# One decode step of attention beside a gated MLP: keys loaded three tiles ahead of values, and the stages spread over more iterations

## The chip, the cores and the metric

The kernel runs on one core of one Trainium2 chip. The core has a matrix engine (PE, whose weight loads the profile lists apart as PEld), a vector engine (DVE), a scalar engine (ACT), a general engine (POOL, hardly used here) and SP, the queue that issues the transfers. Sixteen DMA engines move data between the chip's memory (HBM) and the core's own memory (SBUF). PE writes its results to a second memory, PSUM.

The metric is the device time of one execution in microseconds. The kernel before has a median of 708.93 us over three runs (703.95 to 710.58).

## What is computed

```
x  = A_x                       # 4 batches, 1 token, D = 640
xn = layernorm(x)
q  = xn @ wq                   # 32 heads of 128 numbers
s  = q . k_cache * 128**-0.5   # for each batch and head: 4096 keys
p  = softmax(s)
o  = p . v_cache               # for each batch and head: 4096 values
A  = o @ wo
z  = gelu(xn @ w_in)           # 1728 columns, two halves of 864
z2 = layernorm(second half of z)
g  = w_sp * z2 + b_sp          # the sequence has length 1, so w_sp is one number
B  = (first half of z * g) @ w_out
out = x + A + B
```

All inputs are bf16. The two caches are 4 x 32 x 4096 x 128 numbers each, 268.4 MB together, and each number is used once. The weights are small beside them: wq and wo 5.2 MB each, w_in 2.2 MB, w_out 1.1 MB.

## The kernel before

**Tiles.** The work on the caches is cut into `NT` = 64 tiles. Tile i is one batch `b = i % 4` and one pair of heads `hp = i // 4`. Its keys lie in SBUF as 128 partitions x `NC` = 64 positions x 128 numbers (2 MB): the lower 64 partitions hold the first head, the upper 64 the second. Its values lie the same way. Key tiles, value tiles and, at the start, the three parts of wq all take their place from one pool of `KV_SLOTS` = 7 slots (line 16).

**One tile goes through these stages.**

- `stage_q` (L362): two matmuls spread the two rows of q over the partitions, and ACT copies the result (`qbc`).
- `products` (L380), twice, for a half of 32 positions each: DVE multiplies keys by q (L385). In the second half alone (`FOLDED`, L54) DVE then adds the upper 64 of the 128 products to the lower 64 (L394, "folding").
- `sums` (L398), twice: PE adds up groups of `RW` = 16 products by matmuls with an identity matrix, 512 columns each (L404): eight of them for the first half, four for the folded one. `row_sums` (L413), twice: DVE reduces the remaining 16 to one score (L414).
- The chain for the maximum: `lane_max` (DVE), `turn_max` (PE transposes), `head_max` (DVE, one maximum for each head), `spread_max` (L442; two matmuls, one for each head, with the constant `halves`, spread the two maxima over the partitions).
- `exps` (L454): ACT copies the maximum, and computes the exponentials of both heads and their sums.
- `weighted` (L470): 64 matmuls with the values as weights and the exponentials as the moving operand, "p.v" in what follows.

After every fourth tile (all batches of a head pair) come `group_den` (L488), `group_norm` (L497) and `group_proj` (L504, four matmuls with wo into the output's sum, `out_ps`).

**The order.** For PE, DVE and ACT the order of the instructions is written out by hand, in the loop of lines 529 to 551. Iteration i holds the products and sums of tile i, the maximum and the exponentials of tile i-1, and p.v of tile i-2. Each engine works through its own list in order, and waits at an instruction until that instruction's inputs are there.

**The loads** are all issued by SP, in the order of the program. `load_to(2 * i + KV_AHEAD)` (L531, with `KV_AHEAD` = 6) issues key and value tiles in turn: k0, v0, k1, v1, and so on. At iteration i these are k(i+2), which takes the slot that p.v of tile i-2 leaves, and v(i+2), which takes the slot of k(i-1). `load_wo` (L130) loads 640 KB of wo, enough for two head pairs, into one of two buffers. It is issued at iterations 1, 9, 17 and so on (L532). From iteration 9 on, the buffer that it takes is in use until the projection at the end of the following iteration, and SP waits in between.

At the start SP issues x, the two single numbers w_sp and b_sp (L77, L79), wq in three parts (L85), k0, v0, k1, v1, w_in (L139), w_out (L140) and the first part of wo.

**The query** (L203 to L216): eight groups of five matmuls, each with the 4 columns of xn as weights and 512 columns of wq as the moving operand, and a copy by ACT for each group.

**The gated MLP** hangs on single iterations (L351 to L356): the product with w_in in six parts of 15 matmuls at iterations 5 to 10 (`gmlp_z`; each has 96 columns of w_in, nine numbers apart, as weights, L239), the gelu at 11, the layer norm and the gate at 12, the product with w_out at 13. The nine chunks are of `FHC` = 96 columns, and w_out lies in SBUF as 96 partitions x 9 rows, so that each partition's rows are contiguous in HBM.

Of the kernel before, what the change touches and what calls it, by code (L numbers as in the profile page):

```python
# [9 lines left out]
FP32 = mybir.dt.float32  # L10
# [6 lines left out]
KV_AHEAD = 6  # L17
# [3 lines left out]
def kernel(  # L21
# [31 lines left out]
    RW = 16  # L53
    FOLDED = (1,)  # L54
    FHC = 96
    NFC = Fh // FHC
# [19 lines left out]
    wsp_bf = const.tile([1, 1], BF16)  # L76
    nc.sync.dma_start(out=wsp_bf[:], in_=B_w_sp[0:1, 0:1])  # L77
    bsp_bf = const.tile([1, 1], BF16)
    nc.sync.dma_start(out=bsp_bf[:], in_=B_b_sp[0:1].rearrange("(a b) -> a b", a=1))  # L79
# [30 lines left out]


    loads = []
    for i in range(NT - 2):
        loads += [("k", i), ("v", i)]
    loads += [("k", NT - 2), ("k", NT - 1), ("v", NT - 2), ("v", NT - 1)]
    n_loaded = [0]

    def load_to(n):
        while n_loaded[0] < min(n, len(loads)):
            what, i = loads[n_loaded[0]]  # L120
            if what == "k":
                load_k(i)
            else:
                load_v(i, 4 if i == NT - 1 else 1)
            n_loaded[0] += 1
# [4 lines left out]
    def load_wo(j):  # L130
        if j < H // HQ:
            wo_tiles[j] = wop.tile([P, HQ, D], BF16, name="wo")
            nc.sync.dma_start(out=wo_tiles[j][:], in_=wo_v[j])
# [20 lines left out]

    halves = const.tile([1, 2, P], FP32)
    nc.vector.memset(halves[:], 0.0)
    for hh in range(2):
        nc.vector.memset(halves[:, hh, hh * HALF : (hh + 1) * HALF], scale_qk)
# [44 lines left out]
    q_rows = const.tile([Bsz, HD], BF16)  # L203
    N0 = 512
    for j in range(HD // N0):
        q_ps = ps_m.tile([Bsz, N0], FP32, tag="m")
        for c in range(DC):
            t, i = wq_parts[c]
            nc.tensor.matmul(  # L209
                out=q_ps[:],  # L210
                lhsT=xnT[:, c, :],
                rhs=t[:, i, j * N0 : (j + 1) * N0],
                start=(c == 0),
                stop=(c == DC - 1),
            )
        nc.scalar.copy(out=q_rows[:, j * N0 : (j + 1) * N0], in_=q_ps[:])  # L216

# [12 lines left out]
    gm = {}  # L230

    def gmlp_z(k0, k1):
        if "z" not in gm:
            gm["z"] = ps_pv.tile([FHC, NZC, Bsz], FP32, tag="pv", name="zT")
        zT = gm["z"]
        w = w_in_sb[:].rearrange("p c (t f k) -> p c t k f", t=2, k=NFC)
        for k in range(k0, k1):
            for c in range(DC):
                nc.tensor.matmul(  # L239
                    out=zT[:, k, :],  # L240
                    lhsT=w[:, c, k // NFC, k % NFC, :],
                    rhs=xnT[:, c, :],
                    start=(c == 0),
                    stop=(c == DC - 1),
                )

    def gmlp_gelu():
        zz = work.tile([FHC, NZC, Bsz], FP32, name="zz")
        nc.vector.tensor_copy(out=zz[:], in_=gm["z"][:])
        gw = work.tile([FHC, NZC, Bsz], FP32, name="gw")  # L250
# [101 lines left out]
    for i in range(6):  # L352
        gmlp[5 + i] = lambda k0=3 * i: gmlp_z(k0, k0 + 3)
# [233 lines left out]
```

## Time and profile before

| | |
|---|---|
| median of three runs | 708.93 us (703.95 to 710.58) |
| the profiled execution | 699.59 us |
| its span, first to last instruction | 697.8 us |
| mean granted PE clock | 0.687 |
| busy: PE, DVE, ACT | 514.5, 482.1, 94.0 us |
| read from HBM | 282.24 MB |

The profile shows one execution. Its span leaves out 1.8 us that lie around the first and the last instruction. The parts that are used below are the shares of busy time; the span in 40 slices (a digit is the busy share in tenths, 9 is 90% or more; GB/s is what the DMA engines moved); the chain of work that ended last; the groups of instructions (line, engine, operation, output <- inputs, shapes, count, then the busy time and the mean of one in ns, then the engine's idle time just ahead of them and what ended most of it); the windows, which give each engine's busy time in a stretch of the span; the waits of the SP queue; and the order of time (start, duration, engine, line, operation, and in square brackets the idle time before it and what ended that).

Busy matmuls overlap in the pipeline, so that their mean duration is longer than the distance from one to the next.

### The profile page before, as it was taken

To read this page: it belongs to the slowest core of one execution; us is meant where nothing else is said; L and a number is where in the kernel's file an instruction comes from. 1 tells how busy PE (TensorE), PEld (TensorE's weight loads), DVE (VectorE), ACT (ScalarE), POOL (GpSimd) and SP (SyncE) were. 2 spreads that over 40 slices of the span, in tenths; PEclk is the share of its full clock that TensorE was granted. 3 is DMA by queue.
4 is the path that set the end of the run, shared out by engine and by line. 5 is a ranking of instruction groups with operands and counts; after the bars stand their busy time and mean duration, and the time that the engine had idled before them with its cause. 6 is when DMAs were issued, how large, how long until landed. Compare 5 with 4: busy or idle time off the path is not lost.

```text
span 697.8 us, 12619 instructions
## 1 busy us (share of the span) xinstructions
PE 514.5 (74%) x5601; PEld 291.5 (42%) x5601; DVE 482.1 (69%) x516; ACT 94.0 (13%) x400; POOL 1.4 (0%) x12
## 2 busy tenths in 40 slices
PE   3737689897697677686767858677676858778786
PEld 0213356564354344342444434344343424444354
DVE  1437667575779668676676857776697776769683
ACT  1210101012111101110110111011011101101111
POOL 0000000000000000000000000000000000000000
PEclk9965566665577758565586755767577665767656
DMA  8999999969999999999999999999999999999991
GB/s 351 431 368 423 427 425 428 425 265 425 427 428 425 399 429 426 427 426 401 429 427 425 397 424 428 426 427 390 428 428 425 429 385 429 425 429 426 425 420 47
DMA packets 23850, 283.06 MB, mean 406 GB/s; under 512 B 2316, under 2 KB 6420, under 8 KB 6932
## 3 DMA queue, kind: packets, MB, share of 16 engines
q1 hardware_dynamic: 23796, 282.26, 96.2%
q8 instruction: 44, 0.72, 0.4%
q14 instruction: 10, 0.08, 0.0%
HBM read 282.24 MB, written 0.01 MB: 404 GB/s over the span
## 4 chain that ended last, share of the span: by engine, by line
DMA 57%; PE 27%; DVE 14%; ACT 1%; issue 1%; SPq 1%; DVEq 0%
DMA k_nat<-in_A_k_cache_dram 55%; PE s_ps L404 15%; DVE prod L385 10%; PE pv L477 4%; PE zT L239 2%; DMA wq<-in_A_wq_dram 2%; PE nb_ps L445 2%; PE q_ps L209 1%; DVE prod L394 1%; PE out_ps L509 1%; DVE s_sb L414 1%; PE out_ps L343 1%; PE den L490 0%; ACT pm L461 0%; DVE nm L433 0%
## 5 line engine op out<-in xcount | busy, mean ns | idle before, releaser
L404 PE MATMUL s_ps<-prod,ident 128*128 128x512 bf16 x768 | 292.5, 542 | 112.7 <-DVE prod L385 112.6
L385 DVE TENSOR_TENSOR prod<-k_nat,qbc 128x4096 bf16<-128x4096 bf16 x128 | 291.5, 2278 | 107.4 <-DMA k_nat<-in_A_k_cache_dram 85.9
L404 PEld LDWEIGHTS <-ident 128*128 128x128 bf16 x768 | 90.7, 126 | 261.9 <-issue 240.8
L477 PEld LDWEIGHTS <-v_nat 128*128 128x128 bf16 x4096 | 116.8, 99 | 18.8 <-issue 12.8
L477 PE MATMUL pv<-pm,v_nat 128*128 128x2 bf16 x4096 | 114.2, 165 | 0.2 <-ACT pm L461 0.2
L414 DVE TENSOR_REDUCE s_sb<-s_ps 128x32 f32<-128x512 f32 x128 | 86.7, 677 | 3.9 <-PE s_ps L404 3.9
L445 PE MATMUL nb_ps<-nm,halves 1*128 1x1 f32 x256 | 47.5, 286 | 51.8 <-DVE nm L433 39.5
L378 ACT CAST qbc<-qbc_ps 128x128 bf16<-128x128 f32 x64 | 17.0, 266 | 477.8 <-PE qbc_ps L370 477.8
L394 DVE TENSOR_TENSOR prod<-prod 128x2048 bf16<-128x2048 bf16 x64 | 78.4, 1225 | 2.2
L445 PEld LDWEIGHTS nb_ps<-nm,halves 1*128 1x128 f32 x256 | 42.9, 235 | 60.7 <-issue 31.7
L461 ACT ACTIVATE pm<-s_sb,nb 64x64 bf16<-64x64 f32 x128 | 46.7, 365 | 2.9
L433 DVE TENSOR_REDUCE nm<-mT 1x2 f32<-1x128 f32 x64 | 17.6, 275 | 40.9 <-PE mT L428 40.7
L494 DVE RECIPROCAL rden<-den 128x8 f32<-128x8 f32 x16 | 3.3, 208 | 46.3 <-PE den L490 46.3
L461 ACT ACTIVATION_READ_ACCUMULATOR pm<-s_sb,nb 64x1 f32 x128 | 23.6, 185 | 0.0
L457 ACT COPY nb<-nb_ps 128x1 f32<-128x1 f32 x64 | 10.2, 159 | 95.3 <-PE nb_ps L445 95.3
L428 PE MATMUL mT<-ident_f,m 128*1 128x128 f32 x64 | 18.7, 292 | 0.0
L209 PE MATMUL q_ps<-wq,xnT 128*4 128x512 bf16 x40 | 13.5, 502 | 6.8 <-DMA wq<-in_A_wq_dram 6.6
L509 PE MATMUL out_ps<-wo,o_n 128*4 128x320 bf16 x64 | 17.4, 418 | 0.3 <-DVE o_n L499 0.3
L239 PEld LDWEIGHTS <-w_in_sb 128*96 128x96 bf16 x90 | 16.5, 268 | 2.5 <-issue 2.5
L370 PE MATMUL qbc_ps<-q_rows,ident 4*64 4x128 bf16 x128 | 16.3, 252 | 0.5 <-ACT q_rows L216 0.5
L239 PE MATMUL zT<-xnT,w_in_sb 128*96 128x4 bf16 x90 | 15.9, 307 | 0.0
L423 DVE TENSOR_REDUCE m<-s_sb 128x1 f32<-128x64 f32 x64 | 14.1, 220 | 2.2
(69 smaller groups left out, 69.8 us busy)
## 6 DMA issues: line engine op xcount, KB each, us to landing
k_nat<-in_A_k_cache_dram SPq DMA_DIRECT2D x64, 2048.0 KB, 21.5
v_nat<-in_A_v_cache_dram SPq DMA_DIRECT2D x63, 2048.0 KB, 17.9
wo<-in_A_wo_dram SPq DMA_DIRECT2D x8, 640.0 KB, 5.7
wq<-in_A_wq_dram SPq DMA_DIRECT2D x2, 2048.0 KB, 11.7
w_in_sb<-in_B_w_in_dram SPq DMA_DIRECT2D x1, 2160.0 KB
v_nat<-in_A_v_cache_dram SPq DMA_DIRECT2D x4, 512.0 KB, 13.0
w_out_sb<-in_B_w_out_dram SPq DMA_DIRECT2D x1, 1080.0 KB
wq<-in_A_wq_dram SPq DMA_DIRECT2D x1, 1024.0 KB, 13.7
```

What stands on the lines that cost most here:

```text
L209: nc.tensor.matmul(out=q_ps[:], lhsT=xnT[:, c, :], rhs=t[:, i, j * N0 : (j + 1) * N0], start=(c == 0), stop=(c == DC - 1),)
L239: nc.tensor.matmul(out=zT[:, k, :], lhsT=w[:, c, k // NFC, k % NFC, :], rhs=xnT[:, c, :], start=(c == 0), stop=(c == DC - 1),)
L385: nc.vector.tensor_tensor(out=t[:], in0=k_tiles[i][:, cs, :], in1=qbcs[i][:, None, :].to_broadcast([P, NH2, Dh]), op=ALU.mult,)
L394: nc.vector.tensor_tensor(out=t[:, :, 0:hd], in0=t[:, :, 0:hd], in1=t[:, :, hd:Dh], op=ALU.add)
L404: nc.tensor.matmul(out=s_ps[:], lhsT=ident[:], rhs=t[:, :, g * RW : (g + 1) * RW], start=(g == 0), stop=(g == n - 1),)
L414: nc.vector.tensor_reduce(out=scores[i][:, half * NH2 : (half + 1) * NH2], in_=sums_ps.pop((i, half))[:], axis=AX.X, op=ALU.add,)
L428: nc.tensor.transpose(out=mT[:], in_=maxes[i][:], identity=ident_f[:])
L433: nc.vector.tensor_reduce(out=nm[:], in_=maxes[i][:].rearrange("a (h p) -> a h p", h=2), axis=AX.X, op=ALU.max, negate=True,)
L445: nc.tensor.matmul(out=nb_ps[:], lhsT=halves[:, hh, :], rhs=maxes[i][:, hh : hh + 1], start=(hh == 0), stop=(hh == 1),)
L461: nc.scalar.activation(out=pm[ps, :, hh], in_=s_sb[ps, :], func=ACT.Exp, bias=nb[ps, :], scale=scale_qk, accum_out=a[ps, hh, b : b + 1],)
L477: nc.tensor.matmul(out=pvs[hp][:, :, b], lhsT=v_nat[:, c, :], rhs=pm[:, c, :], start=(c == 0), stop=(c == NC - 1),)
L509: nc.tensor.matmul(out=out_ps[:, oh, 0:NOH], lhsT=o_n[:, hh, :], rhs=wo_tiles[j][:, 2 * half + hh, oh * NOH : (oh + 1) * NOH], start=False ...
```

## The change

It does the following.

- **Loads.** The order of the tiles becomes k0, k1, k2, k3, v0, k4, v1, and so on, with `K_LEAD` = 3. At iteration i, SP issues k(i+3) and v(i). k(i+3) takes the slot of v(i-4), and v(i) the slot of k(i). The last value tile comes in three parts (a half and two quarters) and not in four quarters.
- **Stages.** p.v of tile i-4 stands in iteration i, in place of tile i-2. The maximum across lanes of tile i-1 stays in iteration i; `spread_max` and the exponentials of tile i-2 move to its beginning. The group stages move back with them, and the loop gets one more iteration.
- **Both halves are folded**, `RW` becomes 8, and both halves' sums go into one PSUM tile: 16 matmuls of 256 columns for a tile, and one `row_sums` over 64 scores in place of two over 32.
- **`spread_max`** is one matmul that spreads both maxima to all partitions, and each half of the exponentials takes its own column.
- **The query** has wq as weights: 160 matmuls with 128 columns of wq as weights and the 4 columns of xn as the moving operand, into one PSUM tile, and one copy by DVE. `stage_q` takes its weights from that copy and moves the identity matrix.
- **The gated MLP** is cut into seven chunks of 128 columns (the last of 96), with contiguous weights, and into pieces that hang on iterations 1 to 15, one on each: 70 matmuls with w_in, the tanh, the gelu, the sums, the variance, the gate's factors, their spreading, the gate, and seven pieces with w_out.
- **wo** is loaded at iterations 1, 3, 14, 22 and so on.
- **The start.** w_in comes behind k0, w_out behind k2; w_sp and b_sp come ahead of w_out. w_out lies in SBUF as 128 partitions x 7 rows, each row by itself in HBM (1280 bytes).

```diff
-KV_AHEAD = 6
+KV_AHEAD = 5
+K_LEAD = 3
...
-    RW = 16
-    FOLDED = (1,)
-    FHC = 96
-    NFC = Fh // FHC
+    RW = 8
+    FW = P
+    NFC = -(-Fh // FW)
+    NFF = Fh // FW
+    FT = Fh - NFF * FW
...
-    loads = []
-    for i in range(NT - 2):
-        loads += [("k", i), ("v", i)]
-    loads += [("k", NT - 2), ("k", NT - 1), ("v", NT - 2), ("v", NT - 1)]
+    loads = [(load_k, i) for i in range(K_LEAD)]
+    for i in range(NT):
+        if i + K_LEAD < NT:
+            loads.append((load_k, i + K_LEAD))
+        loads.append((load_v, i))
...
+    load_to(1)
+    nc.sync.dma_start(out=w_in_sb[:], in_=B_w_in.rearrange("(p c) n -> p c n", c=DC))
+    load_to(3)
+    nc.sync.dma_start(out=wsp_bf[:], in_=B_w_sp[0:1, 0:1])
+    nc.sync.dma_start(out=bsp_bf[:], in_=B_b_sp[0:1].rearrange("(a b) -> a b", a=1))
+    nc.sync.dma_start(
+        out=w_out_sb[:, 0:NFF, :],
+        in_=B_w_out[0 : NFF * FW].rearrange("(k p) n -> p k n", p=FW),
+    )
+    nc.sync.dma_start(out=w_out_sb[:FT, NFF, :], in_=B_w_out[NFF * FW : Fh])
     load_to(4)
-    nc.sync.dma_start(out=w_in_sb[:], in_=B_w_in.rearrange("(p c) n -> p c n", c=DC))
-    nc.sync.dma_start(out=w_out_sb[:], in_=B_w_out.rearrange("(p c) n -> p c n", c=NFC))
-    load_wo(0)
...
+    q_ps = ps_m.tile([P, H, Bsz], FP32, tag="m", name="q_ps")
+    for h in range(H):
         for c in range(DC):
             t, i = wq_parts[c]
             nc.tensor.matmul(
-                out=q_ps[:],
-                lhsT=xnT[:, c, :],
-                rhs=t[:, i, j * N0 : (j + 1) * N0],
+                out=q_ps[:, h, :],
+                lhsT=t[:, i, h * Dh : (h + 1) * Dh],
+                rhs=xnT[:, c, :],
                 start=(c == 0),
                 stop=(c == DC - 1),
             )
-        nc.scalar.copy(out=q_rows[:, j * N0 : (j + 1) * N0], in_=q_ps[:])
+    qT = const.tile([P, H, Bsz], BF16)
+    nc.vector.tensor_copy(out=qT[:], in_=q_ps[:])
...
+    pieces = [gmlp_z, gmlp_tanh, gmlp_gelu, gmlp_sums, gmlp_var, gmlp_ac, gmlp_spread]
+    pieces += [gmlp_gate] + [lambda k=k: gmlp_out(k) for k in range(NFC)]
...
+        hd = Dh // 2
+        nc.vector.tensor_tensor(
+            out=t[:, :, 0:hd], in0=t[:, :, 0:hd], in1=t[:, :, hd:Dh], op=ALU.add
+        )
         prods[i, half] = t
...
-        nb_ps = ps_m.tile([P, 1], FP32, tag="m", name="nb_ps")
-        for hh in range(2):
-            nc.tensor.matmul(
-                out=nb_ps[:],
-                lhsT=halves[:, hh, :],
-                rhs=maxes[i][:, hh : hh + 1],
-                start=(hh == 0),
-                stop=(hh == 1),
-            )
+        nb_ps = ps_m.tile([P, 2], FP32, tag="m", name="nb_ps")
+        nc.tensor.matmul(
+            out=nb_ps[:], lhsT=scale_row[:], rhs=maxes[i][:], start=True, stop=True
+        )
...
-        for i in range(NT + 4):
+        for i in range(NT + K_LEAD + 2):
             load_to(2 * i + KV_AHEAD)
-            if i % 8 == 1:
-                load_wo(i // 8 + 1)
+            if i in (1, 3):
+                load_wo(i // 2)
+            elif i % 8 == 6 and i > 8 and (i + 2) // 8 < H // HQ:
+                load_wo((i + 2) // 8)
             at(i, products, 0)
-            at(i - 1, row_sums, 1)
+            at(i - 2, spread_max)
+            at(i - 2, exps)
+            group(i - 3, group_den)
+            at(i - K_LEAD - 1, weighted)
+            at(i - 1, row_sums)
             at(i - 1, lane_max)
-            group(i - 3, group_norm)
+            group(i - K_LEAD - 2, group_norm)
             at(i, sums, 0)
-            group(i - 2, group_den)
-            at(i - 2, weighted)
             at(i - 1, turn_max)
-            at(i + 2, stage_q)
             at(i, products, 1)
             at(i - 1, head_max)
-            at(i - 1, spread_max)
-            at(i - 1, exps)
+            at(i + 2, stage_q)
             at(i, sums, 1)
-            at(i, row_sums, 0)
-            group(i - 3, group_proj)
-            if i in gmlp:
-                gmlp[i]()
+            group(i - K_LEAD - 2, group_proj)
+            if 1 <= i <= len(pieces):
+                pieces[i - 1]()
```

More of the change, by code (lines that the diff above doesn't have):

```diff
@@ L119, in load_to @@
         while n_loaded[0] < min(n, len(loads)):
[L120 to L124, printed above, removed]
+            fn, i = loads[n_loaded[0]]
+            fn(i)
             n_loaded[0] += 1
@@ L230, with gmlp_z, gmlp_tanh @@
     gm = {}
[L232 to L250, printed above, removed]
+    gm_names = ("zz", "gw", "gt", "gz")
+    for name in gm_names:
+        gm[name] = const.tile([P, 2, NFC, Bsz], FP32, name=name)
+    nc.gpsimd.memset(gm["zz"][:], 0.0)
+    gm["sq"] = const.tile([P, NFC, Bsz], FP32, name="sq")
+    gm["st"] = const.tile([1, 5 * Bsz], FP32, name="st")
+    gm["ac"] = const.tile([1, 2 * Bsz], FP32, name="ac")
+    gm["yT"] = const.tile([P, NFC, Bsz], BF16, name="yT")
+    def gmlp_z():
+        zT = ps_pv.tile([P, 2, NFC, Bsz], FP32, tag="pv", name="zT")
+        gm["zT"] = zT
+        for t in range(2):
+            for k in range(NFC):
+                w = FW if k < NFF else FT
+                f0 = t * Fh + k * FW
+                for c in range(DC):
+                    nc.tensor.matmul(
+                        out=zT[:w, t, k, :],
+                        lhsT=w_in_sb[:, c, f0 : f0 + w],
+                        rhs=xnT[:, c, :],
+                        start=(c == 0),
+                        stop=(c == DC - 1),
+                    )
+    def gmlp_tanh():
+        zz, gw = gm["zz"], gm["gw"]
+        nc.vector.tensor_copy(out=zz[:, :, 0:NFF, :], in_=gm["zT"][:, :, 0:NFF, :])
+        nc.vector.tensor_copy(out=zz[:FT, :, NFF, :], in_=gm["zT"][:FT, :, NFF, :])
         nc.vector.tensor_tensor(out=gw[:], in0=zz[:], in1=zz[:], op=ALU.mult)
@@ L255, in gmlp_gelu @@
         nc.vector.tensor_tensor(out=gw[:], in0=gw[:], in1=zz[:], op=ALU.mult)
-        gt = work.tile([FHC, NZC, Bsz], FP32, name="gt")
         nc.scalar.activation(
-            out=gt[:], in_=gw[:], func=ACT.Tanh, scale=math.sqrt(2.0 / math.pi)
+            out=gm["gt"][:], in_=gw[:], func=ACT.Tanh, scale=math.sqrt(2.0 / math.pi)
         )
+    def gmlp_gelu():
+        gt, gz = gm["gt"], gm["gz"]
         nc.vector.tensor_scalar(
@@ L286, in gmlp_ln, with gmlp_var @@
                 )
-        st = work.tile([1, 5 * Bsz], FP32, name="st")
+        gm["s_ps"] = s_ps
+    def gmlp_var():
+        st = gm["st"]
         mean_t = st[:, 0:Bsz]
@@ L362, in stage_q @@
     def stage_q(i):
-        if i >= NT:
-            return
         hp, b = divmod(i, Bsz)
-        q_ps = ps_m.tile([P, Dh], FP32, tag="m", name="qbc_ps")
+        qb_ps = ps_m.tile([P, Dh], FP32, tag="m", name="qbc_ps")
         for hh in range(2):
-            h = 2 * hp + hh
             nc.tensor.matmul(
-                out=q_ps[hh * HALF : (hh + 1) * HALF, :],
-                lhsT=ident[:Bsz, b : b + 1].to_broadcast([Bsz, HALF]),
-                rhs=q_rows[:, h * Dh : (h + 1) * Dh],
+                out=qb_ps[hh * HALF : (hh + 1) * HALF, :],
+                lhsT=qT[:, 2 * hp + hh, b : b + 1].to_broadcast([P, HALF]),
+                rhs=ident[:],
                 start=True,
@@ L377, in stage_q @@
         qbcs[i] = small.tile([P, Dh], BF16, name="qbc", bufs=3)
-        nc.scalar.copy(out=qbcs[i][:], in_=q_ps[:])
+        nc.scalar.copy(out=qbcs[i][:], in_=qb_ps[:])
     def products(i, half):
-        if half == 0:
-            scores[i] = small.tile([P, NC], FP32, name="s_sb")
         cs = slice(half * NH2, (half + 1) * NH2)
@@ L410, in sums, with row_sums @@
             )
-        sums_ps[i, half] = s_ps
-    def row_sums(i, half):
+    def row_sums(i):
+        scores[i] = small.tile([P, NC], FP32, name="s_sb", bufs=3)
         nc.vector.tensor_reduce(
-            out=scores[i][:, half * NH2 : (half + 1) * NH2],
-            in_=sums_ps.pop((i, half))[:],
-            axis=AX.X,
-            op=ALU.add,
+            out=scores[i][:], in_=sums_ps.pop(i)[:], axis=AX.X, op=ALU.add
         )
```

148 lines of the change are left out of this document (68 added, 80 removed).

## The prediction

> **What bounds the kernel now.** I read the page from its top: the shares, the slices, the chain. Then I cut the span into windows along the dips of the DMA rate, and last looked at who held the SP queue in each dip.
>
> ```profile
> PE 514.5 (74%) x5601; PEld 291.5 (42%) x5601; DVE 482.1 (69%) x516; ACT 94.0 (13%) x400; POOL 1.4 (0%) x12
> ...
> DMA  8999999969999999999999999999999999999991
> GB/s 351 431 368 423 427 425 428 425 265 425 427 428 425 399 429 426 427 426 401 429 427 425 397 424 428 426 427 390 428 428 425 429 385 429 425 429 426 425 420 47
> DMA packets 23850, 283.06 MB, mean 406 GB/s; under 512 B 2316, under 2 KB 6420, under 8 KB 6932
> ...
> HBM read 282.24 MB, written 0.01 MB: 404 GB/s over the span
> ...
> DMA 57%; PE 27%; DVE 14%; ACT 1%; issue 1%; SPq 1%; DVEq 0%
> ...
> k_nat<-in_A_k_cache_dram SPq DMA_DIRECT2D x64, 2048.0 KB, 21.5
> ```
>
> No compute engine is full (PE 74%, DVE 69%), the DMA row is 9 nearly everywhere, and over half of the chain is a key tile arriving. The plateau of the GB/s row is 425 to 429; I use 427. At it the 282.24 MB take 661.0 us, so the span of 697.8 holds 36.8 us in which the stream isn't at its plateau. A tile of keys or values is 2048 KB, 4.91 us, so an iteration (one of each) brings 9.82 us of stream. The windows say where the 36.8 us lie. Columns: stretch, its length, busy time and count of PE, PEld, DVE, ACT, POOL, granted clock, DMA share, GB/s.
>
> ```profile
> 40.00:46.00 6.00, 1.54 (x8) 0.92 (x9) 0.79 (x2) 2.32 (x6) 0.00 (x0) 0.70 0.97 245
> 46.00:147.00 101.00, 78.62 (x755) 48.69 (x755) 65.85 (x65) 10.40 (x48) 0.00 (x0) 0.60 1.01 425
> 147.00:154.00 7.00, 6.64 (x93) 5.17 (x92) 4.81 (x6) 1.30 (x6) 0.00 (x0) 0.91 0.12 26
> 154.00:233.00 79.00, 63.76 (x736) 36.26 (x735) 60.43 (x78) 13.53 (x52) 0.00 (x0) 0.70 1.01 427
> 233.00:236.00 3.00, 2.79 (x41) 1.66 (x40) 2.96 (x4) 0.00 (x0) 0.00 (x0) 0.91 0.71 263
> ...
> 315.00:318.00 3.00, 2.72 (x7) 0.99 (x7) 2.96 (x4) 0.00 (x0) 0.00 (x0) 0.50 0.81 271
> ...
> 396.00:399.00 3.00, 2.64 (x22) 1.22 (x21) 2.96 (x4) 0.00 (x0) 0.00 (x0) 0.77 0.64 205
> ...
> 478.00:481.00 3.00, 2.79 (x30) 1.50 (x30) 2.97 (x4) 0.00 (x0) 0.00 (x0) 0.78 0.66 210
> ...
> 560.00:563.00 3.00, 2.65 (x27) 1.39 (x27) 2.96 (x4) 0.00 (x0) 0.00 (x0) 0.80 0.60 193
> ...
> 682.00:685.00 3.00, 2.63 (x71) 2.13 (x69) 2.67 (x4) 0.00 (x0) 0.00 (x0) 1.00 0.20 78
> 685.00:697.80 12.80, 7.85 (x146) 5.82 (x146) 2.32 (x7) 2.48 (x11) 0.00 (x0) 0.60 0.01 2
> ```
>
> A dip's loss is its length times (1 - rate/427). That is 2.6 us at 40:46, 6.6 at 147:154, and 1.15, 1.10, 1.56, 1.52 and 1.64 (7.0 in all) in five short dips some 82 us apart. Another 2.5 us go at 682:685, and 12.8 us pass after the last byte. What holds the queue in the six inner dips is in the SP queue's own waits and its order of time:
>
> ```profile
> SPq L133 <- PE out_ps L509: 83.6, 6, 15.2
> ...
> 151.88 0.38 SPq L133 DMA_DIRECT2D wo<-in_A_wo_dram  x1
> ```
>
> Six times `load_wo` stands in front of the next key load and waits up to 15.2 us for a projection to give up its `wo` buffer. At iteration i the queue behind an arriving key tile holds v(i), k(i+1), v(i+1): 14.7 us, so a 15 us wait just empties it. At 147:154 it is emptied wholly, because the zT chunks have filled PE just there.
>
> **The change, part by part.**
>
> *wo loads.* They move to iterations 1, 3, 14, 22 and so on; the buffer that each takes was last read by the projection two iterations earlier, so the wait goes. The 640 KB remain. What such a load costs behind a full queue shows the second one, which was queued behind four tiles and passed at 66:69:
>
> ```profile
> 66.00:69.00 3.00, 3.00 (x8) 1.05 (x8) 2.93 (x4) 0.00 (x0) 0.00 (x0) 0.50 1.04 388
> ```
>
> There 0.27 us are lost. So the five short dips give back 7.0 - 5 x 0.27 = 5.6 us. Bounds: 0 (if the dip is the packets' own) to 7.0.
>
> *gMLP spread out, zT before the first p.v.* With `wo` no longer waiting, 147:154 gives back 6.6 - 0.27 = 6.3 us. The 70 new pairs of `gmlp_z` all fall into iteration 1. Nearest rows: 15 old pairs take 2.60 us (173 ns each, weights read with a stride of 9), 64 p.v pairs with contiguous weights 1.85 us (29 ns; row below). So it is 2.0 to 12.1 us; I take 2.0, as the new weights are contiguous. Either lies beside loads already queued. The DVE pieces, a few tenths each, go one per iteration into its idle time.
>
> ```profile
> 97.34 2.60 PE L239 MATMUL zT<-xnT,w_in_sb 128*96 128x4 bf16 x15
> ...
> 691.51 1.85 PE L477 MATMUL pv<-pm,v_nat 128*128 128x2 bf16 x64
> ```
>
> *wq as weights.* The last part of wq and the first product stand in the order of time:
>
> ```profile
> 16.32 1.01 PE L209 MATMUL q_ps<-wq,xnT 128*4 128x512 bf16 x2 [0.62 <-DMA wq<-in_A_wq_dram]
> ...
> 27.13 4.49 DVE L385 TENSOR_TENSOR prod<-k_nat,qbc 128x4096 bf16<-128x4096 bf16 x2 [21.54 <-ACT qbc L378]
> ```
>
> 160 pairs start at 16.3 us and take 160 x 29 ns = 4.6 us, or 27.7 us by the zT row: q is ready at 21 or 44, against 26 now, and the first product starts a microsecond later. Cover: k0, w_in, k1, k2, w_out and k3 need no slot of wq; with wq they are 5.2 + 4 x 2.1 + 2.2 + 1.1 = 16.9 MB, 40 us of stream. v0 is the first load that waits for q. By the lower bound nothing is lost, by the upper about 4 us. I take 0.
>
> *Keys three ahead, p.v four later.* When k(i) arrives, v(i-3), k(i+1), v(i-2), k(i+2), v(i-1) are queued: 24.6 us. k(i+3) takes the slot of v(i-4), released by p.v at the head of iteration i; v(i) takes that of k(i), released by the second product some 7 us in (two products, a fold, a reduction and a maximum). SP is in order, so v(i) also waits behind k(i+3); the queue never falls below 24.6 - 7 = 17.6 us. Before, k(i+2) waited for p.v(i-2), behind a product, eight sums and 64 pairs (2.3 + 3.6 + 1.9 us): 14.7 - 7.8 = 7 us were left. So a stall of any engine under 17 us no longer reaches the stream.
>
> *Both halves folded, one row reduction.*
>
> ```profile
> L404 PE MATMUL s_ps<-prod,ident 128*128 128x512 bf16 x768 | 292.5, 542 | 112.7 <-DVE prod L385 112.6
> L385 DVE TENSOR_TENSOR prod<-k_nat,qbc 128x4096 bf16<-128x4096 bf16 x128 | 291.5, 2278 | 107.4 <-DMA k_nat<-in_A_k_cache_dram 85.9
> ...
> L414 DVE TENSOR_REDUCE s_sb<-s_ps 128x32 f32<-128x512 f32 x128 | 86.7, 677 | 3.9 <-PE s_ps L404 3.9
> ...
> L394 DVE TENSOR_TENSOR prod<-prod 128x2048 bf16<-128x2048 bf16 x64 | 78.4, 1225 | 2.2
> ```
>
> DVE gains a fold (1.225 us) and loses one of two reductions of 512 numbers (0.677): +0.55 us an iteration, 482.1/64 = 7.5 becomes 8.1 us. Its cover is the 9.82 us of stream; without that cover it would cost 64 x 0.55 = 35 us. PE's sums go from 12 matmuls of 512 columns to 16 of 256, a third fewer columns. `spread_max` needs one matmul for two. Both are off the path; 0.
>
> *w_out, wsp, bsp.* w_out's rows become 864 packets of 1280 bytes in place of 96 large ones. The 40:46 dip holds w_out and the first wo, and costs 2.6 us now. At the plateau its 1.1 MB take 2.6 us, at the 193 GB/s of the worst dip 5.7. Bounds: -2.3 (the dip, less 0.27 for wo, is w_out's and goes) to +3.1 (the dip is none of w_out's, and the new packets crawl). I take 0, between them. The Trainium skill's page "DMA: Bandwidth & Descriptors" (Specifications) puts the size from which a transfer runs at line rate at 512 B. By that the new packets cost nothing and 2.3 us would come off the sum; the 388 GB/s of the wo load at 66:69 agrees more than the dips do. The two tiny loads leave the head of the queue:
>
> ```profile
> 1.14 0.22 SPq L77 DMA_DIRECT2D wsp_bf<-in_B_w_sp_dram  x1
> ...
> 1.70 1.30 SPq L85 DMA_DIRECT2D wq<-in_A_wq_dram  x3
> ```
>
> wq is issued at 1.14 and not at 1.70: -0.5 us. w_in is moved ahead of k1 and w_out ahead of k3, within a stream that is full either way.
>
> *The end.*
>
> ```profile
> 680.56 2.28 DVE L385 TENSOR_TENSOR prod<-k_nat,qbc 128x4096 bf16<-128x4096 bf16 x1
> ...
> 693.62 1.23 PE L509 MATMUL out_ps<-wo,o_n 128*4 128x320 bf16 x4 [0.26 <-DVE o_n L499]
> ...
> 695.42 0.29 SPq L556 DMA_DIRECT2D out_dram<-res  x1
> ```
>
> Now the last tile's product, sums, maximum and exponentials all follow the last byte. After the change the last keys lie four tiles (19.6 us) ahead of it, and what follows is the last quarter of p.v (16 of 64 pairs, 0.46 us) and the stretch from p.v's end at 693.36 to 697.8 (4.4 us). From the last byte to PE's start I put 0.5 us (0 to 2). That is 5.4 for 12.8: -7.4. Late next is only the projection and the output.
>
> **Sum:** -0.5 - 5.6 - 6.3 - 7.4 = -19.8 us; the span becomes 678.0. The profiled execution took 699.59, 1.8 above its span, and becomes 679.8. The runs shown have a median of 708.93, 9.3 above the profiled execution. If that excess is a slower stream it stays (689.1). If it is more of the same stalls, the deeper queue swallows it (679.8). No row tells which; the stream gets most of the weight, as it is the bound: 688.
>
> **Rivals.** *(1) The wo dips stay*, because they are the packets' own cost and not an empty queue. For it: they sit exactly at the loads, and 6420 packets are under 2 KB. Against: 66:69. Price: 5.6 + 1.3 us, so 695.
>
> *(2) The start starves the stream.* If 128-column weights load as slowly as zT's, q comes at 44 us and `gmlp_z` holds PE for 12 us; v0, on which the slots turn, is late. For it: the only row with 4 moving columns is the slow one. Against: p.v's 29 ns. Price 4 to 15 us, so 692 to 703.
>
> *(3) Slower: PE becomes the bound.* The sums' 256-column matmuls read runs of 8 numbers in place of 16, and may cost as much apiece as 512 columns. Rows at half clock:
>
> ```profile
> 655.26 1.89 PE L477 MATMUL pv<-pm,v_nat 128*128 128x2 bf16 x64
> 657.01 0.37 PE L428 MATMUL mT<-ident_f,m 128*1 128x128 f32 x1
> 657.31 0.31 PE L370 MATMUL qbc_ps<-q_rows,ident 4*64 4x128 bf16 x2
> 657.98 1.01 PE L445 MATMUL nb_ps<-nm,halves 1*128 1x1 f32 x4 [0.36 <-ACT qbc L378]
> 658.93 1.89 PE L404 MATMUL s_ps<-prod,ident 128*128 128x512 bf16 x4
> ```
>
> 16 x 0.47 + 1.89 + 0.37 + 0.31 + half of 1.01 + 0.4 (projection, a quarter) = 11.0 us an iteration, over the 9.82. Then 64 x 11.0 + 22 before the first product + 5 = 731 of span, some 742 by the median. It decides from (697.8 - 27)/64 = 10.5 us an iteration, that is 0.44 us a matmul; with halved matmuls even at half clock it is 7.3. The granted clock is 0.50 to 0.91 in the windows above. The Trainium skill's page "TensorE: Matmul & The Clock Gate" (Part 1: The HAM clock gate) says that an idle stretch of some 3.4 us sends PE back to half clock, so a PE with less to do spends more time there. It speaks against the change; the 7.3 us are at that clock already.
>
> **Chances.** Forecast 0.66, rival 1 0.12, rival 2 0.12, rival 3 0.08, something unseen 0.02. One per cent is 7.1 us, about what a measurement of this kernel can tell from no change: faster is below 701.8. The forecast and rival 1 lie below that but for 0.03, rival 2 by nearly half, so faster 0.80, same 0.10, slower 0.10. The range runs from 679 (all of the excess gone) to 701 (rival 1, most of rival 2).
>
> **What would show it.** Right: the DMA row without dips at the wo loads and at 147 us, no SP wait on `out_ps`, a plateau still near 427, q ready near 21 us, and 5 to 6 us behind the last byte. Wrong: a GB/s row below 427 with PE or DVE near full; DVE over 9.8 us an iteration; dips of over 1 us at each wo load; sums of 0.4 us a matmul; a plateau that has itself moved, since every step rests on it.

## The result, and the profile after

The changed kernel takes 680.99 us (median of four runs, 680.82 to 681.20), the kernel before 706.81 us (four runs, 703.95 to 710.58): a ratio of 0.9632, 95% interval 0.9578 to 0.9686. The profiled execution took 680.82 us with a span of 679.0; the sum of the prediction had said 679.8 and 678.0, its forecast for the median 688. Ratios leave out runs that lie over 1.5% above the fastest of their kernel.

The page of the changed kernel: shares, the DMA slices with their rate, and the chain by engine.

```profile
PE 450.9 (66%) x5817; PEld 317.5 (47%) x5817; DVE 518.1 (76%) x515; ACT 89.8 (13%) x393; POOL 1.4 (0%) x13
...
DMA  8999999999999999999999999999999999999994
GB/s 367 426 418 422 419 426 425 426 429 426 427 420 429 422 428 420 429 425 428 425 422 426 428 425 428 419 427 426 428 422 423 426 429 428 421 423 428 428 423 165
...
DMA 70%; DVE 17%; PE 11%; SPq 1%; issue 1%; DVEq 0%
```

The slices of 265, 385 or 390 GB/s are gone; between the first and the last slice nothing is below 418. In the chain DMA went from 57% to 70%, with PE down from 27% to 11%. The same stretches as in the prediction, in the changed kernel (columns as there), and, in the second fence, the first four microseconds of the kernel before:

```profile
0.00:4.00 4.00, 0.00 (x0) 0.00 (x0) 2.05 (x9) 1.43 (x2) 1.44 (x13) 1.00 0.47 141
...
34.00:37.00 3.00, 1.35 (x7) 0.95 (x7) 2.93 (x5) 0.00 (x0) 0.00 (x0) 1.00 0.96 368
40.00:46.00 6.00, 6.00 (x87) 5.07 (x87) 5.93 (x6) 1.18 (x2) 0.00 (x0) 1.00 1.02 429
46.00:147.00 101.00, 71.48 (x847) 49.12 (x846) 84.57 (x97) 17.69 (x71) 0.00 (x0) 1.00 1.01 424
147.00:154.00 7.00, 5.90 (x82) 4.03 (x81) 6.16 (x5) 1.29 (x6) 0.00 (x0) 1.00 1.01 431
...
233.00:315.00 82.00, 55.29 (x696) 38.80 (x694) 64.30 (x61) 10.41 (x48) 0.00 (x0) 0.74 1.01 424
...
396.00:478.00 82.00, 54.20 (x699) 38.35 (x698) 65.61 (x61) 10.68 (x49) 0.00 (x0) 0.54 1.01 425
...
663.00:674.00 11.00, 10.60 (x257) 8.81 (x255) 1.47 (x5) 2.07 (x10) 0.00 (x0) 0.50 0.54 219
674.00:679.00 5.00, 1.81 (x20) 0.84 (x20) 0.65 (x2) 0.41 (x1) 0.00 (x0) 0.50 0.00 1
```

```profile
0.00:4.00 4.00, 0.00 (x0) 0.00 (x0) 2.33 (x11) 1.43 (x2) 1.37 (x12) 1.00 0.35 87
```

The gain of 18.8 us in the span, by the formula of the prediction (length times 1 - rate/427):

| term | predicted | measured in the two traces |
|---|---|---|
| wq issued earlier | -0.5 | -0.5 (54 GB/s more over 4 us) |
| w_out, first wo | 0 | -2.2 (2.6 lost before, 0.4 now, at 34:37) |
| 147:154 | -6.3 | -6.6 |
| the five short dips | -5.6 | -7.0 |
| behind the last byte | -7.4 | -7.8 (12.8 to 5.0) |
| the stream's last microseconds | 0 | +2.9 (5.4 at 663:674 against 2.5 at 682:685) |
| the plateau, 424 to 426 in place of 425 to 428, with the wo loads' own packets in it | 0 | +2.4 (the remainder; the plateau's windows add up to losses of 3.0 us here and 0.7 before) |
| sum | -19.8 | -18.8 |

The prediction charged 0.27 us for each wo load within the two dip rows (-6.3 and -5.6, together -11.9); measured, that cost lies in the plateau's row. The two dip rows and the plateau together make -11.2. The rate of the kernel before is down to 391 GB/s over 674:682 already. These 0.7 us stand in the plateau's row; put to the stream's last microseconds, they would make the two rows +2.2 and +3.1.

That the sum agrees to 1 us is partly luck: w_out (-2.2) and the time behind the last byte (-0.4) came out better than predicted, the stream's last microseconds (+2.9) and the dips with the plateau (+0.7) worse.

### The profile page after: what moved, and what is told of

Its sections match the earlier page's. It is cut to its first block, busy times and chain, and to the rows that moved or that the text cites. A ratio compares the mean times of both kernels' runs of the same rounds, so it can differ in the third digit from the quotient of the medians.

```text
span 679.0 us, 13140 instructions
## 1 busy us (share of the span) xinstructions
PE 450.9 (66%) x5817; PEld 317.5 (47%) x5817; DVE 518.1 (76%) x515; ACT 89.8 (13%) x393; POOL 1.4 (0%) x13
## 4 chain that ended last, share of the span: by engine, by line
DMA 70%; DVE 17%; PE 11%; SPq 1%; issue 1%; DVEq 0%
DMA k_nat<-in_A_k_cache_dram 66%; DVE prod L400 10%; DVE prod L407 5%; PE s_ps L419 4%; PE pv L484 4%; DMA v_nat<-in_A_v_cache_dram 4%; DVE s_sb L429 1%; PE den L497 1%; PE nb_ps L456 1%; DVE m L435 0%; PE out_ps L366 0%; PE out_ps L516 0%; SPq L83 0%; SPq L102 0%; SPq L96 0%
## 5 line engine op out<-in xcount | busy, mean ns | idle before, releaser
L419 PE MATMUL s_ps<-prod,ident 128*128 128x256 bf16 x1024 | 236.2, 409 | 207.5 <-DVE prod L407 206.9
L419 PEld LDWEIGHTS <-ident 128*128 128x128 bf16 x1024 | 139.2, 136 | 266.4 <-issue 208.1
L407 DVE TENSOR_TENSOR prod<-prod 128x2048 bf16<-128x2048 bf16 x128 | 156.7, 1225 | 4.4
L464 ACT COPY nb<-nb_ps 128x2 f32<-128x2 f32 x64 | 10.3, 160 | 287.5 <-PE nb_ps L456 287.5
L456 PEld LDWEIGHTS nb_ps<-nm,scale_row 1*128 1x128 f32 x128 | 31.5, 303 | 27.8 <-issue 27.3
L429 DVE TENSOR_REDUCE s_sb<-s_ps 128x64 f32<-128x512 f32 x64 | 43.0, 672 | 1.8 <-PE s_ps L419 1.8
L456 PE MATMUL nb_ps<-nm,scale_row 1*128 1x2 f32 x128 | 36.9, 355 | 0.0
L440 PE MATMUL mT<-ident_f,m 128*1 128x128 f32 x64 | 26.3, 411 | 0.0
L387 PEld LDWEIGHTS <-qT 128*64 128x64 bf16 x128 | 8.3, 126 | 28.4 <-issue 27.5
L387 PE MATMUL qbc_ps<-ident,qT 128*64 128x128 bf16 x128 | 19.8, 311 | 2.5 <-DVE nm L445 2.1
## 6 DMA issues: line engine op xcount, KB each, us to landing
v_nat<-in_A_v_cache_dram SPq DMA_DIRECT2D x2, 512.0 KB, 25.9
```

The lines of the kernel that those rows point to most:

```text
L387: nc.tensor.matmul(out=qb_ps[hh * HALF : (hh + 1) * HALF, :], lhsT=qT[:, 2 * hp + hh, b : b + 1].to_broadcast([P, HALF]), rhs=ident[:], st ...
L407: nc.vector.tensor_tensor(out=t[:, :, 0:hd], in0=t[:, :, 0:hd], in1=t[:, :, hd:Dh], op=ALU.add)
L419: nc.tensor.matmul(out=sums_ps[i][:, half * NH2 : (half + 1) * NH2, :], lhsT=ident[:], rhs=t[:, :, g * RW : (g + 1) * RW], start=(g == 0), ...
L429: nc.vector.tensor_reduce(out=scores[i][:], in_=sums_ps.pop(i)[:], axis=AX.X, op=ALU.add)
L440: nc.tensor.transpose(out=mT[:], in_=maxes[i][:], identity=ident_f[:])
L456: nc.tensor.matmul(out=nb_ps[:], lhsT=scale_row[:], rhs=maxes[i][:], start=True, stop=True)
```

## The experiments

The first three add parts of the change to the kernel before; all others undo or stress one part of the changed kernel. A run of a variant was compared with runs of the kernel before on the same chip, and the median of the latter was 705.4 (13 runs), 703.95 (one), 704.46 (nine) and 705.16 us (four) in the four sessions. Spans are compared with the one profiled execution of the kernel before (697.8 us, 699.59 as a run), which is faster than all but two of these runs. So differences of spans are smaller than those of the medians, which are 8.4, 6.4 and 12.2 us for the first three.

**1. Only the wo loads moved** (`b_wo`).

```diff
-            if i % 8 == 1:
+            if i % 8 == 3:
                 load_wo(i // 8 + 1)
```

> The kernel before with only the wo loads moved from iterations 8j+1 to 8j+3, behind the projection that frees their buffer. Theory (SP's wait empties the queue): no SP wait on out_ps, the five short dips lose about 5.6 us of their 7.0, and most of the stall at 147:154 goes too; the span falls from 697.8 to 686 to 690, ratio 0.983 to 0.988. Rival (the 1280-byte packets are slow by themselves): the five dips stay at 1.1 to 1.6 us each and move 20 us later, ratio 0.99 to 1.00.

Measured: 696.97 us, ratio 0.9896 (0.983 to 0.9963), span 693.6. Windows of this kernel at two places of the old dips and at a new one, and two waits of SP, the first of them new:

```profile
178.00:193.00 15.00, 11.29 (x97) 6.17 (x97) 11.68 (x13) 2.58 (x7) 0.00 (x0) 0.52 0.81 324
...
313.00:320.00 7.00, 6.64 (x80) 3.97 (x80) 5.00 (x6) 0.27 (x1) 0.00 (x0) 0.50 1.02 435
394.00:402.00 8.00, 4.74 (x82) 3.18 (x80) 5.57 (x5) 1.30 (x6) 0.00 (x0) 0.92 1.01 427
```

```profile
SPq L106 <- PE mT L428: 14.8, 1, 14.8
...
SPq L133 <- DMA wq<-in_A_wq_dram: 4.5, 1, 4.5
```

The five dips are gone, and with them every wait of SP for `out_ps`: it was the wait and not the packets. Where the packets of the moved loads pass, the lowest rates over 3 us are 378 to 402 GB/s, 0.2 to 0.3 us lost each. Rival 1 falls. But the gain is 4.2 us in the span, less than expected (the ratio too just misses its range), because a stall of 15 x (1 - 324/427) = 3.6 us appears at 178:193. There the layer norm and the gate stand in one iteration, behind the six zT chunks, and SP waits 14.8 us for a slot. In the kernel before the stream stops earlier, at 147, and runs at its plateau at this place. Taking away one stall uncovers the next.

**2. Only contiguous chunks of 96 columns** (`b_contig`).

```diff
-        w = w_in_sb[:].rearrange("p c (t f k) -> p c t k f", t=2, k=NFC)
+        w = w_in_sb[:].rearrange("p c (t k f) -> p c t k f", t=2, k=NFC)
...
-    nc.sync.dma_start(out=w_out_sb[:], in_=B_w_out.rearrange("(p c) n -> p c n", c=NFC))
+    nc.sync.dma_start(out=w_out_sb[:], in_=B_w_out.rearrange("(c p) n -> p c n", c=NFC))
```

> The kernel before with only the gMLP's columns taken in contiguous chunks of 96 (and w_out row by row, 864 packets of 1280 bytes, still on 96 partitions). Theory: contiguous weights load as fast as p.v's, 15 zT pairs take 0.4 to 0.6 us in place of 2.6, and the stall at 147:154 shrinks by 2 to 4 us; if the dip at 40:46 came from w_out's large packets it shrinks from 2.6 to 0.4 us, if it came from the 96 partitions it stays. Ratio 0.99 to 0.995. Rival (narrow moving operands are slow whatever the weights): 15 pairs stay at 2.6 us.

Measured: 699.01 us, ratio 0.9923 (0.9884 to 0.9962); the profiled execution's span of 698.1 is no shorter than the 697.8 of before. In the order of time and the windows of this kernel:

```profile
98.34 1.33 PE L239 MATMUL zT<-xnT,w_in_sb 128*96 128x4 bf16 x15
```

```profile
38.00:49.00 11.00, 3.32 (x15) 1.45 (x14) 2.97 (x4) 2.58 (x7) 0.00 (x0) 0.66 1.05 313
145.00:154.00 9.00, 8.01 (x148) 5.48 (x144) 7.72 (x9) 1.57 (x7) 0.00 (x0) 0.99 0.72 271
```

15 pairs take 1.33 us, half of before but not the 0.4 to 0.6 expected: contiguous weights of 96 columns cost 89 ns a pair in five of the six groups (55 in the sixth), those of 128 columns 29 (p.v) and 28 (the query of the changed kernel, 156 pairs in 4.32 us). The new zT takes 2.58 us for 70 pairs, 37 ns on average; ten of these still have 96 columns. The stall at 147 halves (9 x (1 - 271/427) = 3.3 us). The dip at 40:46 stays (11 x (1 - 313/427) = 2.9 us at 38:49) though w_out's packets are now 1280 bytes, as in the changed kernel, which loses 0.4. What is left to tell the two apart is the number of partitions: 96 here, 128 there. Runs 9 and 10 take that up.

**3. Both edits** (`b_both`).

> The kernel before with both edits, loads and stages in the old order. Theory (the gain is the sum of separate stalls): no stall inside the stream, span 683 to 687, and only the 12.8 us behind the last byte are left against the changed kernel; ratio 0.975 to 0.985. Rival (only the longer lead closes the stalls): dips stay, span over 690.

Measured: 693.21 us, ratio 0.9834 (0.977 to 0.9898), span 690.3. Nothing is left inside the stream but the dip at 40:46; the layer norm's place, 178:193, runs at the plateau as well. The expected span was missed by 3 us. What the expectation left out lies at the end: the rate falls over the last 11 us (4.9 us lost, 2.5 at 682:685 before), and 14.3 us in place of 12.8 follow the last byte.

```profile
147.00:154.00 7.00, 7.00 (x92) 4.26 (x90) 4.56 (x6) 0.00 (x0) 0.00 (x0) 0.57 1.01 428
178.00:193.00 15.00, 12.91 (x132) 6.91 (x128) 10.16 (x10) 2.58 (x7) 0.00 (x0) 0.66 1.00 426
...
665.00:676.00 11.00, 10.04 (x157) 6.20 (x155) 9.85 (x9) 1.04 (x5) 0.00 (x0) 0.85 0.58 236
676.00:690.30 14.30, 8.39 (x152) 6.16 (x147) 3.70 (x9) 2.48 (x11) 0.00 (x0) 0.59 0.01 2
```

The rival that only the longer lead closes the stalls falls: the span is at its 690, but the dips are gone. Of the 11.3 us to the changed kernel's span, 14.3 - 5.0 = 9.3 lie behind the last byte.

**4. Keys one tile ahead** (`a_lead1`): the changed kernel with each key tile loaded one tile ahead of the values in place of three, p.v two iterations after the products in place of four (`K_LEAD` sets both), and as many slots.

```diff
-K_LEAD = 3
+K_LEAD = 1
```

> The changed kernel with keys one tile ahead in place of three and p.v two iterations later in place of four; seven slots as before, so the queue is as deep. Theory (the lead of the keys shortens the end and nothing else): the stream keeps its plateau, and the last tile's chain (8 us of products and folds, 7 us of sums, maximum, exponentials and p.v) follows a key tile that comes 9.8 us ahead of the last byte: 4 to 6 us longer, about 685.5. Rival (the lead is what keeps the queue full): dips inside the stream, 690 or more.

Measured: 688.94 us, ratio to before 0.9775 (0.9683 to 0.9867), span 687.0, so 8.0 us over the changed kernel.

```profile
663.00:674.00 11.00, 8.68 (x95) 5.66 (x92) 7.95 (x7) 1.04 (x5) 0.00 (x0) 0.50 0.54 224
674.00:687.00 13.00, 6.84 (x140) 5.49 (x139) 2.04 (x6) 2.48 (x11) 0.00 (x0) 0.50 0.01 2
```

The stream ends at 674 as with three tiles; all of the 8 us lie behind it (13.0 against 5.0). So the lead of the keys, with the later p.v that goes with it, shortens the end and nothing else, as the theory had it. Its size was 8 and not 4 to 6: in PE's order the spreading of tile 62's maximum and its p.v, which waits for the exponentials, stand between the sums of tile 63 (ending at 674.1) and the transpose of its maximum (677.55), and the expectation had left these 3.4 us out.

**5 and 6. A longer wait of SP** (`a_wo6`, `a_wo7`): wo part j at iteration 8j-6, and at 8j-7 in place of 8j-2.

```diff
-            elif i % 8 == 6 and i > 8 and (i + 2) // 8 < H // HQ:
-                load_wo((i + 2) // 8)
+            elif i % 8 == 2 and i > 8 and (i + 6) // 8 < H // HQ:
+                load_wo((i + 6) // 8)
```

> The changed kernel with wo part j issued at iteration 8j-6 in place of 8j-2, two iterations before its buffer is given up. SP then stands for about 2 x 9.8 + 3 = 23 us six times. Theory (the stream loses only what a wait exceeds the queue): behind v(i) the queue holds 17.6 + 2 x 4.9 = 27.4 us, so 4.6 us are left and the time stays at 681 to 683. Rival (a wait of SP costs whatever the queue holds): dips like those before, 1 to 1.6 us six times, 687 to 691.

> The same one iteration earlier still, at 8j-7: SP stands for about 33 us, 5 us more than the 27.4 us that are queued. Theory: six stalls of about 5 us, 705 to 715, and the SP queue waits about 33 us for out_ps six times. If the queue is deeper than worked out, the time stays below 690.

Measured: 683.25 and 706.68 us (one run each), spans 681.5 and 704.9. SP's waits and one of the six stalls, first of `a_wo6`, then of `a_wo7`:

```profile
SPq L125 <- PE out_ps L516: 143.1, 6, 25.1
```

```profile
472.00:480.00 8.00, 7.47 (x89) 4.89 (x88) 6.32 (x5) 1.30 (x6) 0.00 (x0) 0.50 0.88 336
```

```profile
SPq L125 <- PE out_ps L516: 164.8, 6, 27.7
```

```profile
313.00:324.00 11.00, 8.18 (x93) 5.27 (x92) 9.23 (x8) 1.57 (x7) 0.00 (x0) 0.50 0.61 231
```

In `a_wo6` five waits of 23.6 us and one of 25.1, all longer than any wait for `out_ps` in the kernel before, cost 2.5 us of span in all. The count had 27.4 us queued, so nothing should be lost; each of the six places loses 0.6 to 1.0 us all the same, and 1.8 where the wait is 25.1 (474.87; 1.7 in the window above). A wo load by itself accounts for 0.27 of that. So the queue isn't used to its last microsecond; run 8 shows a reason that would fit.

In `a_wo7` the trace has wo one load earlier than in `a_wo6`, and not two, as the program has it: 14 key tiles and 10 value tiles are issued ahead of the first of the six, 14 and 11 in `a_wo6`. So SP waits for 27.5 us on average and not for the expected 33, and one value tile less is queued: 27.4 - 4.9 = 22.5 us. The wait exceeds the queue by 5.0 us, and each of the six stalls costs 4.7 to 5.3 (11 x (1 - 231/427) = 5.0 here), 25.9 us of span in all. The expectation came to about 5 by 33 - 27.4 = 5.6: wait and queue were both off by some 5 us, and the agreement is luck. The rule holds: what decides is by how much the wait exceeds the queued work.

**7. One half folded** (`a_fold1`), so that PE sums the first half with 16 matmuls of 256 columns.

```diff
-        nc.vector.tensor_tensor(
-            out=t[:, :, 0:hd], in0=t[:, :, 0:hd], in1=t[:, :, hd:Dh], op=ALU.add
-        )
+        if half == 1:
+            nc.vector.tensor_tensor(
+                out=t[:, :, 0:hd], in0=t[:, :, 0:hd], in1=t[:, :, hd:Dh], op=ALU.add
+            )
...
-        n = Dh // RW // 2
+        n = Dh // RW // (1 + half)
```

> The changed kernel with only the second half of a tile folded: DVE loses 64 folds of 1.225 us, PE gains 8 matmuls of 256 columns for a tile. Theory (both engines lie under the stream): span 678 to 680, DVE busy 440, PE busy up by some 100. Rival (the fold is part of the gain or DVE is near its bound): more than 2 us either way.

Measured: 682.39 us (one run), span 680.6. DVE is down by 78 us as expected, PE up by only 29 in place of some 100, and the end moves by 1.6 us, a little over the range:

```profile
PE 480.0 (71%) x6329; PEld 354.8 (52%) x6329; DVE 439.9 (65%) x451; ACT 89.7 (13%) x393; POOL 1.4 (0%) x13
```

Neither engine sets the time. Where the 1.6 us come from stays open.

**8. The last value tile in one piece** (`a_onev`).

```diff
-        cuts = (0, 32, 48, NC) if i == NT - 1 else (0, NC)
+        cuts = (0, NC)
```

> The changed kernel with the last value tile in one piece of 16 KB packets. Before the end the DMA rate falls from 425 to about 200 GB/s for some 9 us. Theory (the sixteen DMA engines don't finish together, since some take longer for each packet): the falling rate stays, and the end moves by the 48 p.v pairs that now follow the last byte, 1.3 us later. Rival (the smaller packets of the pieces are the cause): the rate holds to the end, which comes 2 to 3 us earlier.

Measured: 682.56 us (one run), span 680.5, 1.5 us more.

```profile
663.00:674.00 11.00, 9.35 (x209) 7.58 (x207) 1.47 (x5) 2.07 (x10) 0.00 (x0) 0.50 0.51 214
674.00:680.50 6.50, 3.09 (x68) 2.12 (x68) 0.64 (x2) 0.41 (x1) 0.00 (x0) 0.50 0.00 1
```

The falling rate is the same with 16 KB packets (214 against 219 GB/s), so the smaller packets are not the cause. In both kernels the packet records show the sixteen engines stop one by one. In the changed kernel all are at work until 663.5, 11 at 665, 8 from 668.5 to 671.5, and none after 674: about half run out of work 5 to 10 us before the last.

The queue's depth is not the cause either. Run 3, with the old order of the loads, has the same falling rate (236 GB/s over 665:676), and `a_wo7`, with the new order and six stalls, loses far less in its last 11 us of stream:

```profile
688.00:699.00 11.00, 10.08 (x255) 8.46 (x252) 1.47 (x5) 2.07 (x10) 0.00 (x0) 0.50 0.83 342
```

The fall is long where nothing has stopped the stream for some 600 us, and short where it stopped some 120 us before the end (here and in the kernel before). That the engines drift apart while the stream runs, and start level again after a stop, would explain all of these, and also why some engines run dry early in `a_wo6`; it was not measured apart.

**9 and 10. A load on 96 partitions, and on 128** (`a_dum96`, `a_dum128`): four additional loads of 0.983 MB that nobody reads.

```diff
+    dummy = const.tile([96, 8, D], BF16, name="dummy")
...
+            if i in (20, 28, 36, 44):
+                nc.sync.dma_start(
+                    out=dummy[:],
+                    in_=B_w_out[0:768].rearrange("(p c) n -> p c n", c=8),
+                )
```

> The changed kernel with four more loads of 0.983 MB on 96 partitions (packets of 10 KB, read by nobody) at iterations 20, 28, 36 and 44. At the plateau they are 4 x 2.3 = 9.2 us. Theory (a load on 96 partitions is slow, which made the dip of w_out): 2 us more for each, 697 to 699, and four dips of 2 us. Rival (the dip came from something else at the start): 690, no dips.

> The same four additional loads of the same 0.983 MB, now as 128 partitions x 6 rows (packets of 7.7 KB) in place of 96 x 8 (10 KB). Theory (the partitions made those loads slow, not the packets): 4 x 2.3 = 9.2 us over the changed kernel, 689 to 691, no dips of over 0.5 us. Rival (any additional load out of turn costs that much): 700 or more.

Measured: 713.81 us, ratio to before 1.0149 (1.0109 to 1.0189), and 690.02 us, 0.9776 (0.9691 to 0.9862). The window around the first additional load, in `a_dum96` and in `a_dum128`:

```profile
248.00:260.00 12.00, 8.74 (x151) 6.81 (x152) 7.82 (x7) 2.34 (x11) 0.00 (x0) 1.00 1.01 254
```

```profile
248.00:260.00 12.00, 8.66 (x151) 6.72 (x152) 7.74 (x8) 2.34 (x11) 0.00 (x0) 0.50 1.01 427
```

The 128-partition loads cost their bytes: 688.3 - 679.0 = 9.3 us of span for 9.2. The 96-partition loads cost 31.8 us, 8.0 each where their bytes take 2.3. The direction was as expected, the size (2 us more for each) far too small. The rate halves for longer than the load's own bytes take, while the DMA share stays at 1: the engines are busy, and every packet takes longer (the 16 KB packets of keys and values that pass at 252:256 about 1.14 us, and 0.61 beside the 128-partition load). The two loads also differ in the size of their packets (10 and 7.7 KB). That is not what makes the difference: on 96 partitions packets of 1.3 KB (run 2) and of 11.5 KB (the kernel before) dip as well. Why the 96 partitions are slow is not shown.

**11. A tile with more packets for the lower engines** (`a_low8`): value tile 62 as 96 partitions and four loads of 8.

```diff
+        if i == NT - 2:
+            for p0, p1 in ((0, 96), (96, 104), (104, 112), (112, 120), (120, 128)):
+                nc.sync.dma_start(
+                    out=v_tiles[i][p0:p1, :, :], in_=kv_view(A_v_cache, i)[p0:p1, :, :]
+                )
+            return
```

> The changed kernel with value tile 62 loaded as 96 partitions and four loads of 8 partitions. By the Trainium skill's page DMA: Bandwidth & Descriptors (section Why a DMA increments its semaphore by 16 and not by 1) a load of 8 partitions runs on the eight lowest DMA engines alone; so two of the tile's eight packets (16 KB, 1.2 us) go from each of the upper eight to each of the lower eight. Theory (eight engines lag, and they are the upper ones): the end comes 1.2 us earlier. If the lower ones lag: 1.2 us later. If the lag is spread over both, or bound by something else than an engine's own packets: within 0.5 us or later.

Measured: 693.70 us, ratio to before 0.9806 (0.9707 to 0.9905), span 691.1, 12.1 us more.

```profile
654.00:677.00 23.00, 13.56 (x226) 10.16 (x224) 9.42 (x12) 3.10 (x15) 0.00 (x0) 0.50 0.98 217
```

The experiment missed its question: it holds a 96-partition load itself, and from 654 the stream runs at half rate to the end, 23 x (1 - 217/427) = 11.3 us lost. Which engines lag stays open; so does a version that would balance them, which wasn't tried.

**12. The query as before** (`a_q`).

```diff
-                out=q_ps[:, h, :],
-                lhsT=t[:, i, h * Dh : (h + 1) * Dh],
-                rhs=xnT[:, c, :],
+                out=q_ps[:],
+                lhsT=xnT[:, c, :],
+                rhs=t[:, i, j * N0 : (j + 1) * N0],
...
-    qT = const.tile([P, H, Bsz], BF16)
-    nc.vector.tensor_copy(out=qT[:], in_=q_ps[:])
+        nc.scalar.copy(out=q_rows[:, j * N0 : (j + 1) * N0], in_=q_ps[:])
...
```

> The changed kernel with the query as before: xn as weights, 512 columns of wq as moving operand, eight copies by ACT, stage_q from q_rows. Theory (the start is covered by the loads that need no slot of wq): first product at 27 in place of 21.3 us, the time within 0.5 us of 681. Rival (the early query is part of the gain): 3 to 6 us more.

Measured: 681.30 us, ratio to before 0.9631 (0.9537 to 0.9725), the same span of 679.0, though the first product starts 5 us later than in the changed kernel (21.26):

```profile
26.20 2.29 DVE L403 TENSOR_TENSOR prod<-k_nat,qbc 128x4096 bf16<-128x4096 bf16 x1 [20.62 <-ACT qbc L398]
```

wq as weights is worth nothing here. None of the variants is faster than the changed kernel.

## Why the prediction was right, and where its terms were off

**What bounds the kernel.** Right: the stream at its plateau is the floor, and the change works by taking away the places where it stops. The plateau stayed at 424 to 429 GB/s.

**wo loads, zT.** Right in mechanism and size; runs 1 to 3 show them as separate causes. What the prediction didn't see is the layer norm's iteration as the next stall behind zT (run 1). It did no harm here: in run 3, with the shorter zT, that place no longer stalls, and the change spreads this work too.

**Keys ahead, p.v later.** That counting the queued tiles tells what a wait costs: right, by runs 5 and 6, to one or two microseconds a wait. The bound of 17 us itself was not tested, as the waits tried were 23.6 us and more with more tiles queued. The prediction put the end's gain to the lead of the keys; run 4, which takes the lead and the later p.v back together, loses 8.0 us there. 5.4 us were expected behind the last byte, 5.0 were measured. One reading was wrong: not all of the last tile's product follows the last byte in the kernel before. The line shown has its second half start at 680.56, ahead of the stream's end; what follows it is the last sums, the maximum, the exponentials and p.v of the last two tiles.

**wq as weights, both halves folded, one row reduction.** Costed at nothing, under the stream's cover: right (run 12 for wq, run 7 for one of the two folds). The single matmul of `spread_max` and the MLP's pieces behind zT were not undone one by one. Of the 160 pairs of the query 156 took 4.32 us in the trace (4.6 expected for all), `gmlp_z`'s 70 pairs 2.58 (2.0), and DVE's 518.1/64 = 8.1 us an iteration is the number predicted. Rival 2 falls with the 128-column weights. Rival 3 falls too: eight matmuls of 256 columns take 1.86 us, 0.23 each, at half the granted clock:

```profile
662.31 1.86 PE L419 MATMUL s_ps<-prod,ident 128*128 128x256 bf16 x8 [2.21 <-DVE prod L407]
```

The Trainium skill's page "TensorE: Matmul & The Clock Gate" (Part 1: The HAM clock gate) has an idle stretch send PE back to half clock, and the prediction expected more time there. The trace bears that out in its second half alone: the granted clock is 1.00 over 46:147, 0.54 over 396:478 and 0.50 at the end, and its mean over the execution is 0.71, before 0.687. It cost nothing either way: four runs with a mean clock of 0.63 to 0.94 differ by 0.4 us.

**w_out.** The term that was mis-sized: 0 was put for it, between -2.3 and +3.1, and -2.2 came. The prediction looked at the packets' size, and the number of partitions was what mattered (runs 9 and 10). The page "DMA: Bandwidth & Descriptors" of the Trainium skill (Specifications), by which packets of 1280 bytes cost nothing, was the better guide to the packets' size: w_out loses 0.4 us. Run 2 shows that the size alone doesn't settle it, since the same packets on 96 partitions lose 2.9.

**The stream's end.** Not in the sum: the rate falls over 11 us, 2.9 us more than at 682:685 before. It comes with a stream that nothing stops, and not with the deeper queue: run 3 has it with the old order of the loads, and `a_wo7` hardly has it with the new one (run 8).

**From the profiled execution to the median.** Here the prediction lost most: the sum was right to 1 us for the profiled execution, and the 7 us between 688 and 681 are the excess of the runs over it. The prediction left most of that excess standing, because the stream is the bound; its other reading, that the excess is more of the same stalls (679.8), is the one that came. The runs lie within 699 to 711 us for the kernel before, 695 to 701 with the wo loads moved, 691 to 695 with both edits of run 3, and 680.8 to 681.2 for the changed kernel, so the spread goes with the stalls. That the stalls make it is inferred, since no slower execution was traced. The granted clock fits: in the two sessions with 13 and 9 runs of the kernel before, the longer runs tend to have the lower mean clock (correlation -0.72 in both), while the changed kernel's time doesn't follow it.

## What to carry to other kernels

When a stream of loads is the floor, sum its time at the plateau and go through what is over that, stretch by stretch; the waits of the issuing queue say who stops it, and a wait costs about what it exceeds the queued work by, not its length. A load that must wait for a buffer, put in front of the loads that feed the stream, stops all of them: place it behind the work that frees its buffer. If unprofiled runs scatter above the profiled one, the scatter can be a sign of stalls; here it went with them.

## What the runs showed of the hardware that was not expected

A load of 0.983 MB on 96 partitions cost 8.0 us of the stream, on 128 partitions 2.3. While the former ran, all DMA engines were busy (share 1.01) and moved little over half as much (254 against 427 GB/s over 12 us).

The sixteen DMA engines don't finish together: after some 600 us without a stop about half of them were done 5 to 10 us before the last, whatever the size of the last packets and with either order of the loads. Where the stream had stopped some 120 us earlier, the fall took 3 us or so.

A weight load with a matmul of 2 to 4 columns took 28 to 29 ns for 128 contiguous columns, 89 ns (55 in one group of six) for 96 contiguous ones, and 173 to 183 ns for 96 with a step of nine numbers.
